# A layer-scale kernel: gamma's load as ACT's first instruction, x's head rows as its second

## The chip, the cores and the metric

The kernel runs on one core of one Trainium2 chip. The metric is the device time of one execution in microseconds (us), lower is better; the median of several runs is taken. A core has TensorE (PE), VectorE (DVE), ScalarE (ACT), GpSimd (POOL) and SyncE (SP). SP and ACT issue transfers here, each on a queue of its own; the transfers of both run on the same 16 DMA engines.

## The reference

```python
B, S, D = 1024, 16, 512          # x, y: B x S x D, gamma: D, all bf16
def reference(x, y, gamma):
    return x + gamma * y
```

Flattened, x, y and the output have 16,384 rows of 512 elements (16.8 MB each). Two of them are read and one is written: 50.3 MB for two vector operations per element.

## The kernel before

Each of the 128 partitions holds 128 rows of 1 KB. The rows of a partition are counted 0 to 127 and cut in two ways. `BLOCKS = [4, 64, 60]` says how the rows lie in memory: a transfer stays inside a block, and a partition's rows of one transfer are contiguous there (4 KB for rows 0:4, 64 KB for rows 4:68). `PIECES = [8, 16, 44, 52, 8]` says what one vector instruction works on.

All of y stays resident in `y_sb`; it is multiplied in place by gamma, x is added in place, and it is stored from there. x has only 76 rows of room in `x_sb`, so its last two loads go into slots that finished additions have freed.

Transfers follow two hand-written lists, one per queue, worked off in order by `ring`. An entry is an x load (rows, slot), a y load, a store or gamma:

- `SP`: y 0:4, y 4:68, x 4:68, y 68:128, x 68:120, x 120:128.
- `ACT`: x 0:4, gamma, then the stores of rows 4:68, 0:4 and 68:128.

`EARLY` says how many entries of each list are moved to the very top of the program, ahead of the barriers in which all engines meet on entry: two of SP's and one of ACT's. `HOLD = ('y', 0, 4)` names y's head load, and `AHEAD` says how many entries of each list are issued before that queue waits for the head's landing: again two and one. TensorE takes the head's semaphore and then sets one semaphore each for SP, ACT and VectorE.

gamma is one row of 1 KB in `gamma_row`. TensorE spreads it over the 128 partitions by a product with a row of ones (line 152) into `gamma_ps`, and VectorE casts that into `gamma_sb` (line 154). TensorE waits in this order: y's head, the ones, gamma; then for the load in `RELEASE` (x 68:120), after which it lets the stores go.

VectorE works off the list `DVE`: multiply pieces 0, 1, 2 (line 180), add pieces 2, 0, 1 (line 189), multiply 3, 4, add 3, 4. An instruction waits for the loads whose rows it touches. Piece 0 is rows 0:8, so its multiplication needs y 0:4 and y 4:68, and its addition x 0:4 and x 4:68. The loads of the profile's lines 132 (x), 135 (y) and 129 (gamma) and the stores of line 138 are all in `ring`; waits are written by `_take`, line 35.

Of the kernel before, what the change touches and what calls it, by code (L numbers as in the profile page):

```python
# [7 lines left out]

PIECES = [8, 16, 44, 52, 8]


SP = [
    ('y', 0, 4),
    ('y', 4, 68),
# [2 lines left out]
    ('x', 68, 120, 24),  # L17
    ('x', 120, 128, 0),
]
ACT = [('x', 0, 4, 0), ('g',), ('s', 4, 68), ('s', 0, 4), ('s', 68, 128)]  # L20

EARLY = (2, 1)

HOLD, AHEAD = ('y', 0, 4), (2, 1)

RELEASE = ('x', 68, 120, 24)

# [10 lines left out]
def kernel(  # L38
# [36 lines left out]
    y_sb = nc.alloc_sbuf_tensor("y_sb", [P, rows, D], dt).ap()  # L75
    x_loads = [w for w in ACT + SP if w[0] == "x"]
    y_loads = [w for w in SP + ACT if w[0] == "y"]
    stores = [w for w in SP + ACT if w[0] == "s"]
    for loads in (x_loads, y_loads, stores):
# [33 lines left out]
    def ring(eng, what, n_early, n_ahead):  # L113

        known, went = 0, False
        for k, w in enumerate(what):
            kind = w[0]
            if k == n_ahead:
                _take(s_held[eng], 1, eng)
            need = frees(w) if kind == "x" else pieces_of(w[1], w[2]) + list(w[3:]) if kind == "s" else []  # L120
            need = max((order[c] + 1 for c in need), default=0)
            if kind == "s" and not went:
                _take(s_go, 1, eng)
                went = True
            if need > known:
                eng.wait_ge(s_add, need)
                known = need
            if kind == "g":
                i = eng.dma_start(out=gamma_row, in_=gamma.unsqueeze(0)).then_inc(s_gamma, 16)
            elif kind == "x":  # L130
                to = x_sb[:, w[3] : w[3] + w[2] - w[1], :]
                i = eng.dma_start(out=to, in_=rows_of(xf, w[1], w[2])).then_inc(s_load[w], 16)
            elif kind == "y":
                r = slice(w[1], w[2])
                i = eng.dma_start(out=y_sb[:, r, :], in_=rows_of(yf, w[1], w[2])).then_inc(s_load[w], 16)
            else:
                r = slice(w[1], w[2])
                i = eng.dma_start(out=rows_of(of, w[1], w[2]), in_=y_sb[:, r, :]).then_inc(s_out, 16)
            if k < n_early:
                early.append(i.ins)  # L140

    ring(nc.sync, SP, EARLY[0], AHEAD[0])
    ring(nc.scalar, ACT, EARLY[1], AHEAD[1])

# [89 lines left out]
```

## Time and profile before

| | us |
|---|---|
| median of 3 runs (lowest to highest) | 119.69 (119.58 to 119.91) |
| span of the profiled execution, first to last instruction | 118.2 |
| VectorE busy in that span | 70.1 |
| multiplications, 5 instructions | 34.7 |
| additions, 5 instructions | 34.7 |
| matmul that spreads gamma | 0.6 |

The profile gives for the profiled execution its span, not a time of its own on the runs' clock; the runs' median is 1.5 us above the span. The page lists what each engine did in that span, the share of 16 DMA engines that each queue held, and the transfers with the time from issue to landing. A line such as `y_sb<-in_y_dram SPq` is a load of y issued by SP. A releaser in brackets names what ended an idle stretch; "L35" there is a semaphore wait.

| transfer | issued at us | issue to landing us |
|---|---|---|
| y 0:4 (512 KB) | 0.00 | 3.4 |
| y 4:68 (8192 KB) | 0.43 | 23.4 |
| x 0:4 (512 KB) | 0.13 | 4.2 |
| gamma (1 KB) | 3.90 | not given |
| x 4:68 (8192 KB) | 3.71 | 39.5 |
| y 68:128 (7680 KB) | 4.09 | 57.3 |

### The profile page before, as it was taken

What the parts mean: (1) busy time and instruction counts of PE and PEld (TensorE: products, weight loads), DVE (VectorE), ACT (ScalarE), POOL (GpSimd) and SP (SyncE); (2) the same over time, 40 slices, a digit from 0 to 9 for tenths busy, and PEclk for the clock granted to TensorE, in tenths of its full rate; (3) what the DMA queues carried; (4) which work ended last, traced back from release to release, by engine and by line L of the source; (5) the groups of instructions that cost most, each with busy time, mean ns of one, the idle gap of its engine ahead of it and who ended that gap; (6) DMA issues with size and microseconds to landing.
All of it is one profiled execution on the core that took longest, in us unless ns stands there. A gap on an engine that the chain in (4) does not pass through costs nothing. (4 is left out here: it accounts for less than half of the span.)

```text
span 118.2 us, 91 instructions
## 1 busy us (share of the span) xinstructions
PE 0.6 (0%) x1; PEld 0.1 (0%) x1; DVE 70.1 (59%) x12; POOL 0.2 (0%) x4
## 2 busy tenths in 40 slices
PE   0000100000000000000000000000000000000000
PEld 0000000000000000000000000000000000000000
DVE  0000200089999969999999999999999900000000
POOL 0000000000000000000000000000000000000000
DMA  6999889988899879879969696898899889799793
GB/s 248 461 666 399 355 355 399 665 355 355 355 599 466 355 333 624 374 333 499 499 288 576 288 576 288 360 637 355 355 576 488 355 355 510 333 582 416 333 499 166
DMA packets 1442, 50.33 MB, mean 426 GB/s; under 512 B 161, under 2 KB 162, under 8 KB 546
## 3 DMA queue, kind: packets, MB, share of 16 engines
q1 hardware_dynamic: 864, 33.03, 64.8%
q10 hardware_dynamic: 578, 17.30, 33.9%
HBM read 33.56 MB, written 16.78 MB: 426 GB/s over the span
## 5 line engine op out<-in xcount | busy, mean ns | idle before, releaser
L180 DVE TENSOR_TENSOR y_sb<-y_sb,gamma_sb 128x4096 bf16<-128x4096 bf16 (+3 forms) x5 | 34.7, 6981 | 10.9 <-DVEq L35 10.9
L189 DVE TENSOR_TENSOR y_sb<-x_sb,y_sb 128x4096 bf16<-128x4096 bf16 (+3 forms) x5 | 34.7, 6981 | 1.2 <-DVEq L35 1.1
L154 DVE CAST gamma_sb<-gamma_ps 128x512 bf16<-128x512 f32 x1 | 0.7, 692 | 10.2 <-DVEq L35 10.2
L146 DVE MEMSET ones_row<- 1x128 bf16 x1 | 0.2, 165 | 2.0 <-PEq L51 2.0
L152 PE MATMUL gamma_ps<-gamma_row,ones_row 1*128 1x512 bf16 x1 | 0.6, 581 | 11.6 <-PEq L35 11.6
L152 PEld LDWEIGHTS gamma_ps<-gamma_row,ones_row 1*128 1x128 bf16 x1 | 0.1, 101 | 11.6 <-issue 11.6
L218 POOL MEMSET const-bfloat16-1.0<- 128x1 bf16 x1 | 0.1, 101 | 0.0
L218 POOL MEMSET const-uint8-127<- 128x1 uint8 x1 | 0.1, 101 | 0.0
L218 POOL MEMSET const-float32-0.0<- 128x1 f32 x1 | 0.1, 98 | 0.2 <-issue 0.2
L218 POOL MEMSET const-float32-1.0<- 128x1 f32 x1 | 0.1, 98 | 0.0
## 6 DMA issues: line engine op xcount, KB each, us to landing
y_sb<-in_y_dram SPq DMA_DIRECT2D x1, 7680.0 KB, 57.3
out_dram<-y_sb ACTq DMA_DIRECT2D x1, 7680.0 KB, 23.8
x_sb<-in_x_dram SPq DMA_DIRECT2D x1, 6656.0 KB, 21.7
x_sb<-in_x_dram SPq DMA_DIRECT2D x1, 1024.0 KB, 22.0
y_sb<-in_y_dram SPq DMA_DIRECT2D x1, 512.0 KB, 3.4
x_sb<-in_x_dram ACTq DMA_DIRECT2D x1, 512.0 KB, 4.2
out_dram<-y_sb ACTq DMA_DIRECT2D x1, 512.0 KB, 22.3
y_sb<-in_y_dram SPq DMA_DIRECT2D x1, 23.4
```

The source lines that it names most:

```text
L146: nc.vector.memset(ones_row, 1.0).then_inc(s_ones, 1)
L152: nc.tensor.matmul(gamma_ps, ones_row, gamma_row, start=True, stop=True).then_inc(s_ps, 1)
L154: nc.vector.tensor_copy(out=gamma_sb, in_=gamma_ps).then_inc(s_dve, 1)
L180: nc.vector.tensor_tensor(out=yt, in0=yt, in1=g, op=MULT).then_inc(s_dve, 1)
L189: nc.vector.tensor_tensor(out=yt, in0=xt, in1=yt, op=ADD).then_inc(s_add, 1)
L218: nc = _bacc.Bacc("TRN2", target_bir_lowering=False, num_devices=1)
```

## The change

The first two entries of ACT's list trade places, and both counts for ACT go from one to two: gamma's load becomes the first instruction of ACT, x's four head rows its second, both stand ahead of the entry barriers, and ACT waits for y's head only before its first store. The waits of the consumers are as they were.

```diff
-ACT = [('x', 0, 4, 0), ('g',), ('s', 4, 68), ('s', 0, 4), ('s', 68, 128)]
-
-EARLY = (2, 1)
-
-HOLD, AHEAD = ('y', 0, 4), (2, 1)
+ACT = [('g',), ('x', 0, 4, 0), ('s', 4, 68), ('s', 0, 4), ('s', 68, 128)]
+
+EARLY = (2, 2)
+
+HOLD = ('y', 0, 4)
+
+AHEAD = (2, 2)
```

## The prediction

> **What bounds the kernel now.** I read the page first: engine shares, the two DMA rows in 40 slices, the queue shares.
>
> ```profile
> span 118.2 us, 91 instructions
> ...
> PE 0.6 (0%) x1; PEld 0.1 (0%) x1; DVE 70.1 (59%) x12; POOL 0.2 (0%) x4
> ...
> DMA  6999889988899879879969696898899889799793
> GB/s 248 461 666 399 355 355 399 665 355 355 355 599 466 355 333 624 374 333 499 499 288 576 288 576 288 360 637 355 355 576 488 355 355 510 333 582 416 333 499 166
> ...
> q1 hardware_dynamic: 864, 33.03, 64.8%
> q10 hardware_dynamic: 578, 17.30, 33.9%
> ```
>
> No engine is busy for more than 59% of the span, but the two queues (q1 is SP's, q10 is ACT's) together hold the 16 DMA engines for 64.8 + 33.9 = 98.7% of it, 116.7 of 118.2 us. Transfers bound this kernel from end to end. A change is worth what it does to the 1.5 us in which the transfers do not run, or to the bytes per us while they do.
>
> Second view: the stretches of the span, cut finely at the start. Columns: stretch, length, busy time of PE, PEld, DVE, POOL, clock, DMA share, GB/s. A packet is booked where it starts, so a stretch in which many 64 KB packets start shows more than 1 and the next shows 0; only stretches much longer than one such packet give a rate.
>
> ```profile
> 0.00:1.00 1.00, 0.00 (x0) 0.00 (x0) 0.00 (x0) 0.20 (x4) 1.00 0.00 0
> 1.00:2.20 1.20, 0.00 (x0) 0.00 (x0) 0.17 (x1) 0.00 (x0) 1.00 0.92 348
> 2.20:3.64 1.44, 0.00 (x0) 0.00 (x0) 0.00 (x0) 0.00 (x0) 1.00 1.04 418
> 3.64:4.00 0.36, 0.00 (x0) 0.00 (x0) 0.00 (x0) 0.00 (x0) 1.00 7.11 2993
> 4.00:6.08 2.08, 0.00 (x0) 0.00 (x0) 0.00 (x0) 0.00 (x0) 1.00 0.00 0
> ...
> 23.00:78.70 55.70, 0.00 (x0) 0.00 (x0) 53.53 (x9) 0.00 (x0) 1.00 1.00 432
> ...
> 117.30:118.20 0.90, 0.00 (x0) 0.00 (x0) 0.00 (x0) 0.00 (x0) 1.00 0.01 0
> ```
>
> Nothing moves for 1.00 us. From 1.00 to 3.64 the two heads move (y's four rows, then x's four rows, 0.52 MB each): 348 x 1.20 + 418 x 1.44 = 1.02 MB in 2.64 us, 386 GB/s. At 3.64 to 4.00 one 64 KB packet starts on each of the 16 engines (2993 x 0.36 = 1.08 MB): y's rows 4:68. In the undisturbed middle the rate is 432 GB/s.
>
> Third view: the timeline of the first 24 us (start, length, queue, line, what; x2 merges two issues).
>
> ```profile
> 0.00 0.85 SPq L135 DMA_DIRECT2D y_sb<-in_y_dram  x2
> 0.13 0.38 ACTq L132 DMA_DIRECT2D x_sb<-in_x_dram  x1
> ...
> 1.99 0.17 DVE L146 MEMSET ones_row<- 1x128 bf16 x1 [1.99 <-PEq L51]
> 3.71 0.33 SPq L132 DMA_DIRECT2D x_sb<-in_x_dram  x1
> 3.90 0.50 ACTq L129 DMA_DIRECT2D gamma_row<-in_gamma_dram  x1
> ...
> 11.59 0.58 PE L152 MATMUL gamma_ps<-gamma_row,ones_row 1*128 1x512 bf16 x1 [11.59 <-PEq L35]
> 12.32 0.69 DVE L154 CAST gamma_sb<-gamma_ps 128x512 bf16<-128x512 f32 x1 [10.16 <-DVEq L35]
> 23.95 2.29 DVE L180 TENSOR_TENSOR y_sb<-y_sb,gamma_sb 128x4096 bf16<-128x4096 bf16 x1 [10.94 <-DVEq L35]
> ```
>
> The reader is to see two things: gamma is on all partitions at 12.32 + 0.69 = 13.01 us, but VectorE then idles 10.94 us more until y's rows 4:68 are there; and the DMA engines have been fed since 1.00 us by three issues that were made before the entry barriers ended (about 1.99).
>
> **The change, part by part.** The runs' median is 119.69 us and the profiled execution's span 118.2; the 1.5 us between them lie around the span and no view shows them. I make the sum against the span and carry the same 1.5 over.
>
> Gamma's load goes from 3.90 to about 0.13 us, ACT's first slot. It was issued at 3.90 and used at 11.59, 7.7 us later; now it can be used as soon as TensorE has passed y's head (SP goes on at 3.71, so TensorE was through just before). Matmul and cast come up to 7 us earlier, 0.58 and 0.69 us long. Gain for the end: none. The cover is y's rows 4:68, which VectorE waits for till 23.95; gamma could be 10.9 us later than it is and cost nothing.
>
> x's head load keeps its queue but stands behind gamma's issue. That took 0.50 us, and some 0.05 us lie between two issues of one queue (SP's two: 0.85 less 0.37 and 0.42 us in the trace). So x's issue starts at about 0.13 + 0.55 = 0.68, not 0.13, and ends at 1.06, not 0.51. Its rows are first read by the add of piece 0, after the add of piece 2 that starts at 43.45 and takes 11.89 us, so not before 55 us: landing at 25 us instead of 4.3 would cost nothing by itself.
>
> ACT reaches the first barrier at 1.06, where SP's two issues end at 0.85: the barriers end about 0.2 us later, VectorE's memset of the ones goes from 1.99 to 2.2. The next thing after the barriers on SP is its wait for y's head, which let it go at 3.71. That leaves 1.5 us of cover; nothing moves. ACT's own wait for y's head now stands ahead of its first store, whose release came at 77.4, so what is queued behind it (three stores) loses nothing. SP's queue, its hold and its four later loads are untouched.
>
> What is left is the feed of the DMA engines in the first 4 us. Bytes and packets are the same: 50.33 MB. Three things decide: when the first packet starts (y's head, from SP at 0.00; first packet at 1.00), whether there is always a packet ready after it, and the price of the small packets. y's head by itself keeps the engines for 0.52 MB / 386 GB/s = 1.4 us, to about 2.4 us. In the profile x's head came next, issued at 0.13 and running from 2.2. Now two transfers can come next: y's rows 4:68 (issued at 0.43, unchanged) and x's head (0.68). The trace does not show how early y's rows 4:68 could have started, since x's head was in front; it bounds it between 1.0 us after the issue (as for y's head: 1.43) and 3.64. A second bound: the first store, 64 KB packets too, was issued at 77.41 while loads still ran, and in the packet records its first packet starts at 78.73, at most 1.32 us after the issue; by that row y's rows are ready at 0.43 + 1.32 = 1.75. I take this one, as it is the same size of packet, and 1.75 is ahead of 2.4. So no gap: 0 us. If the path that makes the packets is one for both queues and works in order of issue (x's head, issued at 0.13, did run strictly behind y's head and strictly ahead of y's rows 4:68), gamma's 1 KB now sits between y's head and y's rows; its cost there lies between 0 and the 0.50 us of its issue.
>
> Row and rule, first: in the packet records gamma's 1 KB, issued at 3.90, moved at 8.62, in between two of y's 64 KB packets on one engine (each 2.42 us), and its completion at 11.12, one such packet later. So two queues take turns packet by packet once both are full, and x's eight 4 KB packets per engine would now be dealt out among y's eight 64 KB packets. The Trainium skill ("DMA: Bandwidth & Descriptors", Queues, rings and completion order) says an engine goes round the queues but drains a whole packet of some 9 to 17 descriptors before it switches. By the row x's head lands late, near 22 us; by the rule its eight descriptors go as one turn and land near 5 us. The sum is the same by both, since nobody reads x's head before 55 us and the bytes before y's last packet are equal.
>
> Second: the heads ran at 386 GB/s, the middle at 432. 1.02 MB at 432 takes 2.36 us: the start loses 0.28 us in all. If x's half of the small packets now runs among large ones, up to that comes back; s 0:4, four rows too, shows no such loss at 98 us (0.155 us per packet, against 0.16 here), so the loss belongs to the first packets, which remain. I take 0, and 0.28 as the end. Against the change speaks the skill's rule in the same page (Rules for kernel authors) that a transfer under 64 KB is mostly overhead: gamma is 1 KB. [...] The row shows an engine moving it in 0.05 us between two packets that run back to back, so the overhead is a delay of gamma, not of the engine.
>
> Sum: 0 (gamma earlier) + 0 (x later) + 0 (barriers) + 0 (feed; ends -0.3 and +0.9) = 118.2 span, **119.7 us**.
>
> **Rivals.** *The engines run dry at the start (slower).* Place: after y's head, at about 2.4 us. Price: if y's rows 4:68 cannot start before x's head (as in the profile, where they came at 3.64), the next packet waits for x's head, which needed 2.2 - 0.13 = 2.1 us from issue and is issued at 0.68, so 2.75: a gap of 0.35 us; with gamma's 0.50 in the shared path ahead of it, 0.85. All later transfers move by that: 120.0 to 120.6, I take 120.2. For it: the strict order of the three; gamma's issue was longer than x's. Against it: the store's 1.32 us. It decides once y's rows become ready later than 2.4 us.
>
> *The small packets cost less (faster).* The 0.28 us come back, and some of the spread between engines (the first 64 KB packets start over 0.35 us, 3.64 to 4.00, and the slowest engine ends the kernel) with it: 119.4, at most 119.1. Against it: the loss lies in the very first packets.
>
> *The gain on gamma reaches the end.* It would need VectorE to wait for gamma; it waits 10.9 us for y's rows. 2% at most, put under faster.
>
> **How the numbers follow.** 0.3%, 0.36 us, is about what a measurement of this kernel can tell from no change: 119.33 to 120.05 is "no change". My forecast 0.55, spread about 0.2 us to both sides. Engines dry 0.30; half of its prices lie over 120.2. Faster 0.15, mostly 119.1 to 119.35. The range 119.3 to 120.4 leaves out about half of the faster case and a quarter of the slower one.
>
> **What would show it.** Right: first packets at 1.00 as now; DMA share near 1 from 1.00 to 4.00; large packets starting near 2.4 instead of 3.64; the matmul near 4; the first multiply within 0.4 us of 23.95 and the last issue near 94.4. The slower rival: a stretch with DMA share well under 0.9 between 2.2 and 3.6, and the first multiply, the add of piece 2 and the last landing all later by one amount. The faster one: the same points all earlier by one amount. I am wrong altogether if the first packet itself moves from 1.00, or if a later point moves that the start did not.

## The result and the profile after

The changed kernel takes 119.94 us (median of 21 runs, 119.75 to 120.07) against 119.69 for the kernel before (21 runs, 119.58 to 119.91): ratio 1.0019, 95% interval 1.0013 to 1.0025. That is 0.25 us, inside the 0.3% that the prediction called no change, but clear of zero. The profiled execution took 119.94 us by the runs' clock, with a span of 118.6 us.

The page of the changed kernel: same packets, same bytes, same busy times of the compute engines; the DMA row of the 40 slices differs in six digits by one to three tenths, mostly near its two ends.

```profile
span 118.6 us, 91 instructions
...
DMA  9988889988899879979969696898899889798791
...
DMA packets 1442, 50.33 MB, mean 424 GB/s; under 512 B 161, under 2 KB 162, under 8 KB 546
...
q1 hardware_dynamic: 864, 33.03, 64.8%
q10 hardware_dynamic: 578, 17.30, 33.8%
```

The two queues hold 98.6% of a span that is longer by 0.39 us (118.23 to 118.62 in the trace): the DMA engines are still hardly ever out of work. They were busy for longer over the same packets: 117.00 us on the mean of the 16 engines against 116.72, summed over the packet records.

The 0.39 us between the two profiles is more than the 0.25 us between the medians, and that has a reason. In each of the 13 profiles whose own time is on record, the time is 1.32 to 1.33 us above the span (119.94 and 118.62 here). By that the profiled execution of the kernel before took about 119.55 us, an estimate, and was 0.14 us under its median. Differences between the two profiles below may hold up to 0.14 us that the change did not make.

The stretches at the start, columns as before. The first packet still starts at 1.00, but from 1.00 to 2.20 only 277 GB/s start (348 before), and the 64 KB packets now begin between 2.20 and 3.64, not at 3.64.

```profile
1.00:2.20 1.20, 0.00 (x0) 0.00 (x0) 0.00 (x0) 0.00 (x0) 1.00 0.97 277
2.20:3.64 1.44, 0.00 (x0) 0.00 (x0) 0.17 (x1) 0.00 (x0) 1.00 2.07 859
```

The timeline of the start:

```profile
0.13 0.53 ACTq L131 DMA_DIRECT2D gamma_row<-in_gamma_dram  x1
...
0.69 0.37 ACTq L134 DMA_DIRECT2D x_sb<-in_x_dram  x1
2.21 0.17 DVE L148 MEMSET ones_row<- 1x128 bf16 x1 [2.21 <-PEq L53]
3.74 0.33 SPq L134 DMA_DIRECT2D x_sb<-in_x_dram  x1
...
4.33 0.58 PE L154 MATMUL gamma_ps<-gamma_row,ones_row 1*128 1x512 bf16 x1 [4.33 <-PEq L37]
5.06 0.69 DVE L156 CAST gamma_sb<-gamma_ps 128x512 bf16<-128x512 f32 x1 [2.68 <-DVEq L37]
24.34 2.29 DVE L182 TENSOR_TENSOR y_sb<-y_sb,gamma_sb 128x4096 bf16<-128x4096 bf16 x1 [18.59 <-DVEq L37]
```

The first addition and the issue of the first store, in the kernel before and then in the changed one:

```profile
43.45 11.89 DVE L189 TENSOR_TENSOR y_sb<-x_sb,y_sb 128x22528 bf16<-128x22528 bf16 x1 [1.08 <-DVEq L35]
77.41 17.36 ACTq L138 DMA_DIRECT2D out_dram<-y_sb  x3
...
43.80 11.89 DVE L191 TENSOR_TENSOR y_sb<-x_sb,y_sb 128x22528 bf16<-128x22528 bf16 x1 [1.03 <-DVEq L37]
77.79 17.32 ACTq L140 DMA_DIRECT2D out_dram<-y_sb  x3
```

gamma is ready 7.3 us earlier (5.75 against 13.01), and VectorE's idle time before its first multiply grows from 10.94 to 18.59 us by just that much and a little more. The multiply itself is 0.39 us later (24.34 against 23.95). From there on the shift is carried nearly unchanged: the first add starts at 43.80 against 43.45, the first store is issued at 77.79 against 77.41, the span ends 0.39 us later. Nearly the whole difference is made before 24 us.

x's head now lands 23.7 us after its issue at 0.69 (4.2 us in the kernel before). In the packet records its 4 KB packets come in eight rounds of 16, one packet for each engine, from 5.09 us on; the rounds start 2.57 us apart, with a round of y's 64 KB packets between any two.

```profile
x_sb<-in_x_dram ACTq DMA_DIRECT2D x1, 512.0 KB, 23.7
```

### The profile page after: what moved, and what is told of

Its sections match the earlier page's. It is cut to its first block, busy times and chain, and to the rows that moved or that the text cites. A ratio compares the mean times of both kernels' runs of the same rounds, so it can differ in the third digit from the quotient of the medians.

```text
span 118.6 us, 91 instructions
## 1 busy us (share of the span) xinstructions
PE 0.6 (0%) x1; PEld 0.1 (0%) x1; DVE 70.1 (59%) x12; POOL 0.2 (0%) x4
## 6 DMA issues: line engine op xcount, KB each, us to landing
x_sb<-in_x_dram ACTq DMA_DIRECT2D x1, 512.0 KB, 23.7
```

## The experiments

Three theories were tried. A: gamma's small load, among the first issues, stands in the way of y's first small packets. B: x's head, issued 0.55 us later, no longer runs between y's head and y's 64 KB packets, and that costs. C: any small load among the first issues costs, wherever it stands. Each set of runs stood beside the kernel before on its own chip (119.70 to 119.79 there), so the ratios are what is compared. In the edits, `...` stands for entries that stay as they are, and `EARLY` and `AHEAD` are put on one line, without `HOLD`, which never changes.

| kernel | gamma | x's head | us | ratio to before, 95% |
|---|---|---|---|---|
| e1 | early, second on ACT | first on ACT, between | 119.71 | 0.9998 (0.9989 to 1.0007) |
| changed | first on ACT | second on ACT | 119.94 | 1.0019 (1.0013 to 1.0025) |
| e8, the same again | first on ACT | second on ACT | 119.86 | 1.0012 (1.0002 to 1.0021) |
| e3 | first on ACT | held, on ACT | 119.89 | 1.0016 (1.0007 to 1.0025) |
| e4, gamma twice | first on ACT | third on ACT | 119.96 | 1.0021 (1.0012 to 1.0030) |
| e7 | behind the barriers | behind gamma | 119.89 | 1.0009 (1.0000 to 1.0017) |
| e10, the same again | behind the barriers | behind gamma | 119.89 | 1.0014 (1.0005 to 1.0023) |
| e6 | held | third on SP | 119.86 | 1.0007 (0.9999 to 1.0016) |
| e9, the same again | held | third on SP | 119.75 | 1.0002 (0.9993 to 1.0011) |
| e12 | first on ACT | third on SP | 119.83 | 1.0004 (0.9995 to 1.0013) |
| e2 | held, behind x's head | behind the barriers | 124.39 | 1.0391 (1.0377 to 1.0406) |
| e5 | first on ACT | second on SP, between | 120.83 | 1.0057 (1.0031 to 1.0082) |
| e11 | first on ACT | second on ACT, y 4:68 ahead of y 0:4 | 120.19 | 1.0039 (1.0026 to 1.0052) |

**e1, gamma early but behind x's head**

```diff
-ACT = [('g',), ('x', 0, 4, 0), ...]
+ACT = [('x', 0, 4, 0), ('g',), ...]
 EARLY, AHEAD = (2, 2), (2, 2)
```

> ACT issues x's head first and gamma second, both ahead of the barriers; nothing else differs from the kernel before. Theory A (gamma's 1 KB stands in the way of y's first small packets: in the changed kernel they moved at 277 GB/s from 1.00 to 2.20 us, against 348 before): gamma now comes after x's head, y's head is not touched, so 119.7 as before, within 0.1. Theory B (x's head comes too late, so that y's 64 KB packets follow y's head directly and share the engines with x's small packets): x's head is back at 0.13 us, so also 119.7. Theory C (any small load among the first issues costs, wherever it stands): 119.9 to 120.0.

Measured: no difference from the kernel before. The stretches fit that: the two heads run one after the other again, and the 64 KB packets start within some 0.1 us of where they did.

```profile
1.00:2.20 1.20, 0.00 (x0) 0.00 (x0) 0.00 (x0) 0.00 (x0) 1.00 0.85 321
2.20:3.64 1.44, 0.00 (x0) 0.00 (x0) 0.17 (x1) 0.00 (x0) 1.00 1.01 407
3.64:4.00 0.36, 0.00 (x0) 0.00 (x0) 0.00 (x0) 0.00 (x0) 1.00 6.41 2745
```

Theory C is out: a small load among the first issues costs nothing by itself that these runs can tell (0.07% at most by the interval).

**e2, x's head behind the barriers, gamma held behind it**

```diff
 ACT = [('x', 0, 4, 0), ('g',), ...]
-EARLY = (2, 1)
+EARLY = (2, 0)
```

> gamma stays late, behind the landing of y's head, as before; only x's head moves, from ahead of the barriers to just behind them (issue at about 1.9 us). Theory A: 119.7, with y's first packets at 350 GB/s from 1.00 to 2.20. Theory B: 119.9 to 120.0, with the first 64 KB packets between 2.4 and 3.0 us and longer than 2.42 us. Theory C: 119.7.

Measured: 124.39, far outside all three. The timeline of that run has the reason in its first line, and the result in the second:

```profile
31.07 0.58 PE L152 MATMUL gamma_ps<-gamma_row,ones_row 1*128 1x512 bf16 x1 [31.07 <-PEq L35]
...
63.35 2.53 SPq L132 DMA_DIRECT2D x_sb<-in_x_dram  x2
```

x's head was issued at 1.90 us, when y's 64 KB packets were already queued, and took 24.6 us to land; gamma, issued at 3.85, came behind it in the same queue and was used at 31.07. In the packet records x's eight 4 KB packets on an engine start at 7.5, 10.1, 12.7 us and so on: one for each 64 KB packet of the other queue. The first three multiplications moved by 8.9 us (first multiply at 32.85), the adds and the later multiplications by 8.0, so the room for x's next rows came free late: SP issued them at 63.35, not at 55.37, and the engines ran dry:

```profile
60.00:64.00 4.00, 0.00 (x0) 0.00 (x0) 4.00 (x2) 0.00 (x0) 1.00 0.00 0
```

No packet starts in these 4 us; in the kernel before the same stretch moves 426 GB/s.

**e3, gamma first and x's head held; e4, two loads of gamma first**

```diff
 # e3
 ACT = [('g',), ('x', 0, 4, 0), ...]
-EARLY, AHEAD = (2, 2), (2, 2)
+EARLY, AHEAD = (2, 1), (2, 1)
```

> gamma is ACT's first instruction as in the changed kernel; x's head waits for the landing of y's head, so it can't be what delays y's. Theory A: 119.9 to 120.0, y's first packets at some 280 GB/s from 1.00 to 2.20. Theory B: 119.9 to 120.0 too, but with y's first packets at 350 GB/s. Theory C: 119.9.

```diff
 # e4: g2 loads gamma into a row that nobody reads
-ACT = [('g',), ('x', 0, 4, 0), ...]
+ACT = [('g',), ('g2',), ('x', 0, 4, 0), ...]
-EARLY, AHEAD = (2, 2), (2, 2)
+EARLY, AHEAD = (2, 3), (2, 3)
```

> The changed kernel with one more 1 KB load of gamma, into a row that nobody reads, between gamma and x's head on ACT's queue: the dose is doubled, and x's head is issued another 0.55 us later. Theory A and theory C: about twice the loss, 120.1 to 120.2. Theory B: 119.95, as in the changed kernel, since x's head is late in both.

Measured: 1.0016 and 1.0021. Doubling the dose of gamma did not double the loss; that speaks against A. e3 alone tells A from B only by y's first packets; they moved at 352 GB/s from 1.00 to 2.20, as B said, but single executions vary too much there (below) to lean on it.

**e5, x's head between again, but on SP's queue; e6, x's head third on SP, gamma held; e7, both of ACT's loads behind the barriers**

```diff
 # e5, ACT: gamma, early
 SP = [('y', 0, 4), ('x', 0, 4, 0), ('y', 4, 68), ('x', 4, 68, 4), ...]
 EARLY, AHEAD = (3, 1), (3, 1)
 # e6, ACT: gamma, held
 SP = [('y', 0, 4), ('y', 4, 68), ('x', 0, 4, 0), ('x', 4, 68, 4), ...]
 EARLY, AHEAD = (3, 0), (3, 0)
 # e7, SP as before
 ACT = [('g',), ('x', 0, 4, 0), ...]
 EARLY, AHEAD = (2, 0), (2, 2)
```

> gamma stays ACT's first instruction, as in the changed kernel, and x's head goes to SP's queue between y's head and y's rows 4:68, all ahead of the barriers: gamma is early, but the two small heads run one after the other again, before any 64 KB packet. Theory B (the loss comes from y's 64 KB packets following y's head directly, without x's head between): 119.7, first 64 KB packets at 3.6 to 4.0 us. Theories A and C (gamma's early load is what costs): 119.9 to 120.0.

> The other half of the square: gamma waits for the landing of y's head as in the kernel before, and x's head goes to SP's queue behind y's rows 4:68, all three ahead of the barriers. No gamma at the start, but 64 KB packets right behind y's head. Theory B: 119.9, first 64 KB packets at 2.4 to 3.0 us. Theories A and C: 119.7. gamma is alone on ACT's queue and should land near 11 us, so VectorE's first multiply stays where it is.

> Both of ACT's loads are issued just behind the barriers, gamma first (about 1.9 us), x's head second (about 2.4 us). Against the run with x's head at 1.9 us and gamma behind it, which took 124.4 us, only their order in the queue and gamma's wait differ. If that run was slow because gamma, behind x's eight packets per engine in one queue, landed at 31 us and held up all multiplications: 119.9 here, matmul before 8 us, first multiply at 24.1 to 24.4. If it was slow because x's head was late: about 124 again. Theory B on the start: 119.9, theories A and C: 119.7, as gamma is no longer among the first issues.

e5 was a miss for every theory, 120.83 with single runs from 119.82 to 121.73. (The two medians give 1.0088, the ratio on record is 1.0057: with runs this far apart its size is rough.) By putting x's head in front on SP's own queue the edit moved the issue of y's rows 4:68 from 0.43 to 0.89 us, and they came too late: in the packet records of its profile four engines stand idle for 0.17, 0.51, 0.82 and 1.18 us before their first 64 KB packet, the last at 4.98. Its stretches show the tail of late starts, which the kernel before does not have (there all 16 packets start by 4.00):

```profile
3.70:4.20 0.50, 0.00 (x0) 0.00 (x0) 0.00 (x0) 0.00 (x0) 1.00 4.00 1622
4.20:5.00 0.80, 0.58 (x1) 0.10 (x1) 0.00 (x0) 0.00 (x0) 1.00 1.23 410
```

So e5 says nothing on gamma; it shows what the engines running dry at the start looks like. Why the rows came so late is not shown: with the 1.32 us that the prediction read off the first store they would have been ready at 2.21, long before the small packets were through at about 4.

e7 answers e2. With the order in the queue turned round, gamma first, the time falls from 124.4 to 119.9 although x's head is issued even later (2.46 against 1.90). What cost 4.5 us was gamma behind x's head. The edit also drops gamma's wait for y's head, but in the kernel before gamma had that wait and was used at 11.59. (The matmul came at 10.46, not before 8; the first multiply at 24.16 as said.)

```profile
10.46 0.58 PE L152 MATMUL gamma_ps<-gamma_row,ones_row 1*128 1x512 bf16 x1 [10.46 <-PEq L35]
```

e6 came out at 1.0007, between the theories.

**The changed kernel, e6 and e7 once more on one chip, and y's large rows first**

```diff
 # e11, from the changed kernel
-SP = [('y', 0, 4), ('y', 4, 68), ('x', 4, 68, 4), ...]
+SP = [('y', 4, 68), ('y', 0, 4), ('x', 4, 68, 4), ...]
-AHEAD = (2, 2)
+AHEAD = (3, 2)
```

> The changed kernel itself, run again so that it shares a chip and its runs of the kernel before with the next two, and for a second profile of it. 119.9 to 120.0 by all theories. If the slow small packets of y's head (277 GB/s from 1.00 to 2.20 us) belong to the change, they are there again; if they vary from one execution to the next, they may be near 350.

> gamma held behind the landing of y's head, x's head third on SP's queue (so 64 KB packets right behind y's head, and no gamma at the start), the same kernel as the earlier run that took 119.86 against 119.78, now beside the changed kernel. If the missing x head between y's head and the 64 KB packets is the whole loss: equal to the changed kernel. If gamma among the first issues has a part of its own: half of the changed kernel's loss, about 0.1 us above the kernel before.

> Both of ACT's loads just behind the barriers, gamma first, the same kernel as the earlier run that took 119.89 against 119.78, now beside the changed kernel: gamma and x's head keep the changed kernel's order and queue but are not among the first issues. Whole loss from the order of the heads: equal to the changed kernel. A part from gamma among the first issues: half the loss.

> No small packets at the very start: SP issues y's rows 4:68 first and y's head second, then x's rows 4:68 without a wait; only y's rows 68:128 wait for the head's landing. ACT is as in the changed kernel. If the loss of the start lies in small packets being slow there, it goes away and the time falls under the kernel before, 119.4 to 119.6. If any packets that come first are slow, 119.7 to 119.9. If the wait for the head, now landing near 22 us, or the first pieces' rows come too late, over 120.

e10 equals the changed kernel (1.0014 and 1.0012): gamma need not be among the first issues for the loss to be there. e9 does not show it (1.0002). e8 also shows how far single profiles vary: y's head moved at 315 GB/s from 1.00 to 2.20 here and at 277 in the first profile of the same kernel.

e11, the attempt to do better, is slower than both kernels. Without small packets in front, the first 64 KB packets pay at the start. The first stretch holds the 16 first ones, the third the 16 second ones:

```profile
0.90:1.50 0.60, 0.00 (x0) 0.00 (x0) 0.00 (x0) 0.00 (x0) 1.00 5.17 1748
1.50:3.60 2.10, 0.00 (x0) 0.00 (x0) 0.17 (x1) 0.00 (x0) 1.00 0.00 0
3.60:4.60 1.00, 0.00 (x0) 0.00 (x0) 0.00 (x0) 0.00 (x0) 1.00 2.42 1050
```

In the packet records the first ones start at 0.99 to 1.40 and take 2.96 to 3.33 us, median 3.06; all later rounds take 2.42. At both sizes tried, it is what comes first that is slow. By the packet records x's rows 4:68 are complete 0.40 us later than in the kernel before and the last store 0.64 us later. So much of the loss is there by then; the first multiply, at 27.05 because gamma's matmul waits for y's head, now landing late, may have a part in the rest, which was not separated. (Both figures may hold some of the 0.14 us by which the profile of the kernel before lies under its median.)

**e12, gamma first, x's head third on SP**

```diff
 # from e6
 ACT = [('g',), ...]
-EARLY, AHEAD = (3, 0), (3, 0)
+EARLY, AHEAD = (3, 1), (3, 1)
```

> gamma is ACT's first instruction and alone on that queue until the stores; x's head is third on SP's queue, behind y's rows 4:68, so that its small packets never take turns with the 64 KB ones. Against the two runs with the same SP list and gamma held (0.09 and 0.03 us above the kernel before), only gamma's place differs. If gamma among the first issues costs something of its own once 64 KB packets follow y's head: 0.2 us above the kernel before, as in the changed kernel. If the rest of the loss came from x's small packets in turn with the large ones: under 0.1 us.

Measured: 1.0004. gamma's place has no price here either. With e1 that settles it within the intervals, about 0.1%: early gamma has no measurable cost with x's head in its old place and none with x's head on SP.

**What is settled and what is open.** The loss goes with x's head, not with gamma. With x's head ahead of y's 64 KB packets on ACT's queue: none. With x's head on ACT's queue after these packets have begun, so that its small packets take turns with them: 0.09 to 0.21% in six runs, mean 0.15%, one of the six intervals touching zero. With x's head behind y's rows on SP's queue, where there are no turns: 0.02 to 0.07% in three runs, mean 0.04%, each interval with zero in it. By the medians alone the turns would be most of the 0.2 us.

The packet records do not bear that out. From the third round of y's 64 KB packets on, the rounds of the changed kernel start 2.57 us apart: the 2.42 us of one 64 KB packet, the 0.16 of one 4 KB packet and nothing for the turn. From the first to the ninth round of 64 KB packets 20.73 us pass there, and 20.71 in e12, which moves the same packets between without turns. The ninth round of e12 starts as late as that of the changed kernel (23.52 and 23.49 us on the mean of the engines, 23.26 in the kernel before).

What the records do show is a dearer start. Counted per engine as time over the shortest seen, 0.156 us (4 KB) and 2.418 us (64 KB), the heads and the first 64 KB packets cost 0.23 us in the kernel before and 0.21 in e1, but 0.53 and 0.33 in the two profiles of the changed kernel, and 0.33, 0.36 and 0.58 in e6, e9 and e12, which lose hardly any time by their medians. That the start is dearer when 64 KB packets follow y's head directly is in all of these profiles. That most of the time is lost there fits one more count: over eleven profiles, all but e5 and e11, the span grows with the latest start in the tenth round of 64 KB packets (25.92 us before, 26.03 in e1, 26.07 to 26.25 in the others; correlation 0.96). Open are two things: why the same packets take longer there, and why e6, e9 and e12 lose less by their medians than the kernels with turns.

## Why the prediction was right

119.94 lies in the range, and "no change within 0.3%" was the likeliest case. The cause it gave holds: VectorE never waits for gamma, and the transfers bound the kernel from end to end, without a gap that counts. It is not exact: the kernel did get slower, by 0.25 us, where the sum had 0. The 1.5 us that it carried from span to time are 1.32 in every profile with a time of its own; that does not touch the forecast, which starts from the median. Point by point:

- *gamma earlier gains nothing.* Right: 7.3 us earlier, all of it turned into VectorE's wait for y's rows (18.59 us, 10.94 before).
- *x's head later costs nothing by itself.* It was issued at 0.69 (0.68 forecast) and landed 23.7 us after that, at 24.4 (near 22 forecast). The turns packet by packet read off gamma's row hold: one 4 KB packet every 2.57 us on an engine. The rule of the Trainium skill ("DMA: Bandwidth & Descriptors", Queues, rings and completion order), a whole packet of 9 to 17 descriptors in one turn, does not agree with this spacing; by it the eight would have followed each other directly. The landing time alone would not have told the two apart, as the prediction meant it to: if y's eight packets of 64 KB go first as one turn, an estimate by that rule is 2.54 + 8 x 2.42 + 8 x 0.16 = 23.2 us, not 5. No instruction waited for x's head. But its place is what the loss goes with.
- *The barriers and the holds.* Right: memset at 2.21 (2.2 forecast), SP's next issue at 3.74 against 3.71.
- *The feed of the engines, taken at 0, ends -0.3 and +0.9.* Here the sum was off, by 0.25 us: the mis-sized term. There was no gap that counts (DMA share 0.97 in the first stretch); y's rows 4:68 began right behind y's head, as the store's row had said. What the prediction overlooked is that the same packets could take longer. It saw a start loss and asked only whether that would shrink with fewer small packets in front. It grew.
- *Rival, engines dry.* Not in the changed kernel, though all later points moved by about one amount (0.35 to 0.39 us), as that rival had said they would; the DMA share tells the two apart. e5 shows the real thing.
- *Rival, small packets cost less.* Wrong sign. e11 takes the two heads from the start and is 0.39% slower than the kernel before, with its late first multiply in that.

The rule that a transfer under 64 KB is mostly overhead (same page, Rules for kernel authors) speaks of the small transfer itself. As a price for the other transfers it did not show here: two small loads in front of x's head (e4, 1.0021) cost what one did (1.0019 and 1.0012), within the intervals.

## What to carry to other kernels

When the DMA engines are busy for 98.7% of the span, a small load that nobody waits for is worth nothing earlier; ask instead what its issue pushes back, and beside which packets the pushed transfer will now run. Keep a small load that others need out from behind a transfer that takes turns with large packets in the other queue (here the order of two entries in one list was worth 4.5 us, e2 against e7). Before crediting a shift of 0.2 us to a row of one profile, profile the same kernel twice, and look where the profiled execution's own time lies among the runs.

## What the runs showed of the hardware

- Two queues with work took turns one packet each on an engine, 4 KB against 64 KB: the 4 KB packets of one queue came 2.57 us apart beside 64 KB packets of the other (e2, changed kernel), so a 512 KB load took 24.6 us instead of 4.2. The turns themselves cost the engines nothing: 2.57 us is the time of the two packets, 2.42 and 0.16.
- The first packets of the program were slow at both sizes: a 64 KB packet that came first took 3.06 us in the median instead of 2.42 (e11), single first 4 KB packets up to 0.69 instead of 0.16 (changed kernel).
- 64 KB packets issued third on one queue, at 0.89 us, did not follow two small transfers without a gap: up to 1.18 us on one engine (e5). The cause is not shown.
